# Moving the last routing chunk's steps among the first expert list's work, and a table load written ahead of them

## The chip, the cores and the metric

The kernel runs on one core of a Trainium2 chip. The core has five engines that each take their instructions in order: TensorE (PE, with its weight loads as PEld), VectorE (DVE), ScalarE (ACT), GpSimd (POOL) and SyncE (SP, which only issues DMA transfers here). They wait for one another through semaphores. The metric is the device time of one execution in microseconds, lower is better; the median of three runs of the kernel before is 774.65 us (772.66 to 775.27).

## The reference

Three layers run one after the other on 1536 tokens of width 512:

```
scores = q @ k.T / sqrt(64), kept for 4 sink columns and a window of 128
x = softmax(scores) @ v                          # 2 batches, 8 heads, 768 positions
h = x @ w_in;  x = (h - tanh(h)) @ w_out         # 512 -> 2048 -> 512
logits = x @ w_gate + log1p(exp(x @ w_noise)) * noise      # 8 experts
top2 and their softmax weights
for e in experts, k in (0, 1):                   # 512 -> 1024 -> 512 per expert
    out[mask] += weight * (relu(x[mask] @ w1[e]) @ w2[e])
```

## The kernel before, in words

**Attention** goes block by block (12 blocks of 128 tokens, 4 pairs of heads each): scores on PE (L371), masked maxima on DVE (L382), exponentials on ACT (L395), normalising on POOL (L406), transposes (L453) and the product with v (L486) on PE. ACT and DVE split the dense layer's first weights beside it: `split_d` reads the loaded tile `rawi0` on ACT (L215, into `cai0`) and on DVE (L216, L220, L223, L228).

**The dense layer** walks the list `seq` of (group, chunk, unit): `a_l1` (L606) makes a tile `h`, `a_chain` applies Tanh on ACT (L614), subtracts on DVE (L616) and splits in two parts (L619, L621), `a_l2` (L638) adds into the chunk's output. Six chunks of 256 tokens; the first four end early, chunk 4 next, chunk 5 last.

**Routing** is the generator `route(c0, c1)`. Each `next` issues one step: transposes of the chunk's rows (L695), their evacuation (L707), the logits (L720), then on DVE and ACT the noise scale (Exp at L751, Ln at L755), the two largest (L766, L768), the running counts on PE (`pp`, L782 and L785), the softmax weights (Exp at L787), positions and row data, and at the end the scatters of the rows into DRAM `xs` by POOL (L808). The last chunk's generator is `r5`; its steps are pulled by `r(k)` between the units of expert list 0.

**The experts** are lists of tokens gathered from `xs`. List 0 holds tokens of the first four chunks alone, so that its work can start while chunk 5 is still routed; lists 1 to 7 need all chunks. Unit n of a list is `b_l1(n)` (L978, tile `h`), `b_chain(n)` (Relu on ACT at L988, the low part on DVE at L989, tile `hh`) and `b_l2(n)` (L1002). There are two banks for `h`: `b_l1(n + 2)` can start when `b_chain(n)` has read its bank. Units 96 to 103 are list 0 (N1 is 96), 104 on is list 1. Its rows come by SP transfers (L903, `xr<-xs`) that wait for every scatter; DVE transposes them (L943), ACT and DVE split them (L961, L963), and then PE can start `h104`. Expert weights are loaded (`rawi<-wm`) and split on ACT and DVE (L231, L232) beside this.

**What sets the order.** Instructions are written in program order and then placed by a scheduler with priorities, engine by engine. From the last dense unit to unit N1 + 10 the order is pinned as written (`in_order`); before it, the scheduler may move an instruction forward to any place that its dependences allow. The loads of ACT's function tables are not written in this kernel: a pass behind the scheduler puts one ahead of an ACT function that the set then loaded lacks.

Of the kernel before, what the change touches and what calls it, by code (L numbers as in the profile page):

```python
# [71 lines left out]
def kernel(ctx: ExitStack, tc: tile.TileContext, qkv, vsink, w64, wm, wgn, noise, out,  # L72
# [609 lines left out]
    def route(c0, c1):  # L682
# [114 lines left out]
        V.tensor_scalar(rs, dd, 1.0, 1e-9, op0=ALU.add, op1=ALU.add)
        V.reciprocal(rs, rs)
        for c in range(c0, c1):
            x, ms = x2s[c], slice((c - c0) * CB, (c - c0 + 1) * CB)  # L800
            xi = x.bitcast(I32)
            V.tensor_copy(x[:, :, 516], ev[:, 0, ms])
            V.tensor_copy(xi[:, :, 517], sl[:, 0, ms])
            V.tensor_copy(x[:, :, 514], rs[:, ms])
            V.tensor_mul(x[:, :, 515], dd[:, ms], rs[:, ms])

# [161 lines left out]

    def b_l1(n, mid=None):
        e, u, d = b_at(n)  # L970
# [5 lines left out]
        for wa, xa in ((0, 0), (1, 0), (0, 1)):  # L976
            for k in range(4):
                nc.tensor.matmul(h[:, :width(e)], w[:, wa, k * 256 + s * P:k * 256 + (s + 1) * P],  # L978
                                 xg[e][:, k, xa, :width(e)], start=t == 0, stop=t == 11)
                t += 1  # L980
                if mid and t == 8:
                    mid()
# [447 lines left out]
```

## Time and profile before

| | |
|---|---|
| Median of 3 runs | 774.65 us (772.66 to 775.27) |
| The profiled execution's own time | 772.26 us |
| Its span, first to last instruction | 770.0 us |
| Mean granted TensorE clock | 0.979 of full speed |
| PE busy | 723.9 us (94%) |
| DVE / ACT / POOL busy | 475.9 (62%) / 356.3 (46%) / 186.4 us (24%) |
| Attention and first dense units | about 0 to 82 us |
| Dense layer (with the rest of attention) | to 425.6 us |
| List 0 | 425.6 to 456.3 us |
| Lists 1 to 7 and the last small list | 460.2 us to the end |

The profile names each instruction by line, engine, operation and tile; times count from the span's start. A line of the timeline gives start, length, the instruction, how many were merged, and in brackets the engine's idle time just before it with what ended it.

### The profile page before, as it was taken

To read this page: it belongs to the slowest core of one execution; us is meant where nothing else is said; L and a number is where in the kernel's file an instruction comes from. 1 tells how busy PE (TensorE), PEld (TensorE's weight loads), DVE (VectorE), ACT (ScalarE), POOL (GpSimd) and SP (SyncE) were. 2 spreads that over 40 slices of the span, in tenths; PEclk is the share of its full clock that TensorE was granted. 3 is DMA by queue.
4 is the path that set the end of the run, shared out by engine and by line. 5 is a ranking of instruction groups with operands and counts; after the bars stand their busy time and mean duration, and the time that the engine had idled before them with its cause. 6 is when DMAs were issued, how large, how long until landed. Compare 5 with 4: busy or idle time off the path is not lost.

```text
span 770.0 us, 12093 instructions
## 1 busy us (share of the span) xinstructions
PE 723.9 (94%) x4346; PEld 653.0 (85%) x4346; DVE 475.9 (62%) x1203; ACT 356.3 (46%) x785; POOL 186.4 (24%) x219
## 2 busy tenths in 40 slices
PE   6878999999699999999999979999999999999991
PEld 3565788888699999988888979999999999899991
DVE  5998678877587587446467766776646474544221
ACT  4977688776353344234346534444343434332110
POOL 4444355531000000000351231313131313132321
PEclk9999899999899999999999999999999999999996
DMA  7453111006998133000225388756757444444421
GB/s 263 138 178 109 56 51 61 2 1 206 297 287 233 56 110 110 1 1 1 84 112 167 125 237 237 213 164 194 193 186 192 164 155 160 143 139 165 143 84 35
DMA packets 62117, 104.96 MB, mean 136 GB/s; under 512 B 19629, under 2 KB 45869, under 8 KB 55392
## 3 DMA queue, kind: packets, MB, share of 16 engines
q1 hardware_dynamic: 54528, 80.20, 34.9%
q0 software_dynamic: 7376, 22.85, 8.7%
q10 hardware_dynamic: 144, 1.05, 0.3%
q8 instruction: 36, 0.59, 0.3%
q14 instruction: 33, 0.27, 0.1%
HBM read 79.12 MB, written 25.68 MB: 136 GB/s over the span
## 4 chain that ended last, share of the span: by engine, by line
PE 44%; issue 24%; DMA 15%; POOL 6%; DVE 6%; ACT 3%; POOLq 0%; SPq 0%; ACTq 0%; DVEq 0%
PE h L606 16%; PE acc L638 15%; DMA prev<-out,tab 6%; DMA out<-y,tab 5%; PE xb L486 4%; POOL out L1030 4%; PE s L371 3%; DMA rawo<-w 2%; POOL prev L883 2%; PE pt L453 2%; DVE e L382 1%; DMA rawi<-wm 1%; ACT e L395 1%; PE x2p L695 1%; PE y L1002 1%
## 5 line engine op out<-in xcount | busy, mean ns | idle before, releaser
L606 PE MATMUL h<-xT,wi 128*128 128x256 f32 x1152 | 160.9, 287 | 7.9 <-DVE th L616 5.9
L606 PEld LDWEIGHTS h<-xT,wi 128*128 128x128 f32 x1152 | 153.1, 192 | 14.9 <-DVE th L616 6.4
L978 PE MATMUL h<-xg,wi 128*128 128x424 f32 (+1 forms) x768 | 157.6, 354 | 4.0 <-ACT xg L961 3.9
L1002 PE MATMUL y<-hh,wo 128*128 128x424 f32 (+1 forms) x768 | 152.0, 347 | 0.7 <-DVE yt L1016 0.5
L638 PE MATMUL acc<-wo,g 128*128 128x512 f32 x576 | 151.1, 396 | 0.0
L978 PEld LDWEIGHTS h<-xg,wi 128*128 128x128 f32 x768 | 138.6, 190 | 8.7 <-ACT xg L961 5.0
L1002 PEld LDWEIGHTS y<-hh,wo 128*128 128x128 f32 x768 | 139.4, 188 | 4.1 <-DVE yt L1016 0.9
L638 PEld LDWEIGHTS acc<-wo,g 128*128 128x128 f32 x576 | 101.9, 189 | 16.5
L988 ACT ACTIVATE hh<-h 128x424 fp32r<-128x424 f32 (+1 forms) x64 | 32.6, 511 | 149.9 <-PE h L978 147.6
L1030 POOL DMA_INDIRECT out<-y,tab x33 | 41.4, 1255 | 189.7 <-DVE y L1029 189.4
L808 POOL DMA_INDIRECT xs<-x,sl x24 | 26.0, 1085 | 235.7 <-DVE th L616 183.7
L989 DVE SCALAR_TENSOR_TENSOR hh<-h,hh 128x424 fp32r<-128x424 f32 (+1 forms) x64 | 37.0, 578 | 73.9 <-ACT hh L988 69.8
L406 POOL TENSOR_TENSOR e<-e,nm 128x528 f32<-128x528 f32 (+1 forms) x48 | 50.1, 1044 | 81.3 <-DVE nm L404 45.5
L616 DVE TENSOR_TENSOR th<-h,th 128x256 f32<-128x256 f32 x96 | 40.4, 420 | 39.6 <-ACT th L614 37.1
L614 ACT ACTIVATE th<-h 128x256 f32<-128x256 f32 x96 | 36.6, 382 | 59.5 <-PE h L606 56.0
L619 ACT CAST g<-th 128x256 fp32r<-128x256 f32 x96 | 38.7, 404 | 55.0 <-PE acc L638 37.7
L395 ACT ACTIVATE e<-e,nm 128x264 f32<-128x264 f32 (+1 forms) x96 | 47.2, 492 | 22.5 <-DVE nm L382 20.3
L621 DVE TENSOR_TENSOR g<-th,g 128x256 fp32r<-128x256 f32 x96 | 43.2, 450 | 22.3 <-ACT g L619 21.4
L486 PE MATMUL xb<-pT,v 128*128 128x256 f32 x220 | 49.1, 352 | 3.6 <-DVE xT L501 2.2
L232 DVE TENSOR_TENSOR wi<-rawi,wi 128x1024 fp32r<-128x1024 f32 x32 | 39.1, 1223 | 21.6 <-ACT wi L231 21.5
L883 POOL DMA_INDIRECT prev<-out,tab x33 | 35.6, 1080 | 44.0 <-DMA out<-y,tab 34.6
L486 PEld LDWEIGHTS xb<-pT,v 128*128 128x128 f32 x220 | 33.7, 197 | 13.5 <-issue 5.3
(172 smaller groups left out, 888.8 us busy)
## 6 DMA issues: line engine op xcount, KB each, us to landing
rawi<-wm SPq DMA_DIRECT2D x31, 1024.0 KB
rawi<-w SPq DMA_DIRECT2D x8, 1024.0 KB
rawo<-w SPq DMA_DIRECT2D x8, 1024.0 KB
xs<-zrow SPq DMA_DIRECT2D x7, 1040.0 KB
xr<-xs SPq DMA_DIRECT2D x28, 224.0 KB
qr<-qkv SPq DMA_DIRECT2D x23, 256.0 KB
rawc<-wm SPq DMA_DIRECT2D x4, 1024.0 KB
out<-zero POOLq DMA_DIRECT2D x1, 3072.0 KB
```

The lines of the kernel that those rows point to most:

```text
L232: nc.vector.tensor_sub(t[:, 1], r, t[:, 0].bitcast(F32))
L395: nc.scalar.activation(e[:, h], e[:, h], AF.Exp, bias=nm[:, h, 0:1], scale=-1.0, accum_out=nm[:, h, 2:3])
L406: nc.gpsimd.tensor_mul(e, e, nm[:, :, 3:4].to_broadcast([P, 2, C]))
L486: nc.tensor.matmul(o, l, r_, start=t == 0, stop=t == len(todo) - 1)
L606: nc.tensor.matmul(h[:, :CT], w[:, wa, k * 256 + s * P:k * 256 + (s + 1) * P], x[:, k, xa, ts], start=t == 0, stop=t == 11)
L616: nc.vector.tensor_sub(th, h[:, :CT], th)
L621: nc.vector.tensor_sub(g[:, 1], th, g[:, 0].bitcast(F32))
L638: i = nc.tensor.matmul(acc[c][m], g[:, ga, m * P:(m + 1) * P], w[:, wa, s:s + 512], start=first and t == 0, stop=done and t == 2)
L883: nc.gpsimd.indirect_dma_start(out=dst, out_offset=None, in_=src[:rows], in_offset=bass.IndirectOffsetOnAxis(ap=t[:n, m, c:c + 1], axis=0) ...
L978: nc.tensor.matmul(h[:, :width(e)], w[:, wa, k * 256 + s * P:k * 256 + (s + 1) * P], xg[e][:, k, xa, :width(e)], start=t == 0, stop=t == 11)
L1002: nc.tensor.matmul(yacc[e][m][:, :width(e)], w[:, wa, s + m * P:s + (m + 1) * P], g[:, ga], start=u == 0 and t == 0, stop=u == NU2 - 1 and ...
L1030: i = nc.gpsimd.indirect_dma_start(out=out[:, :], out_offset=bass.IndirectOffsetOnAxis(ap=t[:n, m, 1:2], axis=0), in_=y, in_offset=None, b ...
```

## The change

In `route`, the softmax weights and the expert numbers are written before the positions are computed, for every chunk (they came behind). In the stretch of chunk 5, the transposes now stand behind all 12 matmuls of the first `b_l1` (behind 8 before); logits stand after 4 matmuls of the second (8 before); the first `b_chain` comes behind both; the steps of the noise scale, the largest two, the counts and the rest each come one unit earlier; and `b_chain(N1 + 1)` comes behind the step with the weights' Exp. A load of the table set that holds Exp and Ln is written at the start of the last dense unit.

```
@@ -787,22 +787,22 @@
         nc.scalar.activation(dd, dd, AF.Exp)
         yield
 
+        info = [(x2s[c], slice((c - c0) * CB, (c - c0 + 1) * CB)) for c in range(c0, c1)]
         if end:
             V.tensor_scalar(zz, ev, 0.0, float(E), op0=ALU.is_equal, op1=ALU.mult)
             V.tensor_add(ev, ev, zz)
+        V.tensor_scalar(rs, dd, 1.0, 1e-9, op0=ALU.add, op1=ALU.add)
+        V.reciprocal(rs, rs)
+        for x, ms in info:
+            V.tensor_copy(x[:, :, 516], ev[:, 0, ms])
+            V.tensor_copy(x[:, :, 514], rs[:, ms])
+            V.tensor_mul(x[:, :, 515], dd[:, ms], rs[:, ms])
         V.tensor_tensor(o12, o12, ppv[:, None].to_broadcast([P, 2, nb, E]), ALU.mult)
         V.tensor_reduce(pos, o12, axis=AX.X, op=ALU.add)
         sl = gp2.tile([P, 2, nb], I32, tag="sl", name=f"sl{c0}", bufs=2)
         V.scalar_tensor_tensor(sl, ev, float(SEC), pos, op0=ALU.mult, op1=ALU.add)
-        V.tensor_scalar(rs, dd, 1.0, 1e-9, op0=ALU.add, op1=ALU.add)
-        V.reciprocal(rs, rs)
-        for c in range(c0, c1):
-            x, ms = x2s[c], slice((c - c0) * CB, (c - c0 + 1) * CB)
-            xi = x.bitcast(I32)
-            V.tensor_copy(x[:, :, 516], ev[:, 0, ms])
-            V.tensor_copy(xi[:, :, 517], sl[:, 0, ms])
-            V.tensor_copy(x[:, :, 514], rs[:, ms])
-            V.tensor_mul(x[:, :, 515], dd[:, ms], rs[:, ms])
+        for x, ms in info:
+            V.tensor_copy(x.bitcast(I32)[:, :, 517], sl[:, 0, ms])
 
         def scatter(m, k, behind=None):
             i = nc.gpsimd.indirect_dma_start(
@@ -966,7 +966,7 @@
         e, u = divmod(n - N1, NU2)
         return e, u, 8 + e * 4 + u // 2
 
-    def b_l1(n, mid=None):
+    def b_l1(n, mid=None, at=12):
         e, u, d = b_at(n)
         w = wsp["i", d]
         s = u % 2
@@ -978,7 +978,7 @@
                 nc.tensor.matmul(h[:, :width(e)], w[:, wa, k * 256 + s * P:k * 256 + (s + 1) * P],
                                  xg[e][:, k, xa, :width(e)], start=t == 0, stop=t == 11)
                 t += 1
-                if mid and t == 8:
+                if mid and t == at:
                     mid()
 
     def b_chain(n):
@@ -1235,6 +1235,8 @@
     PAIR = N1 - 12
     for n in range(-3, N1):
         marks["a", n] = mark()
+        if n == N1 - 1:
+            nc.scalar.preload_act_table_set("natural_log_exp_and_others")
         g, c, u, d = a_at(max(n, 0))
         ch = a_chain(n + 2) if 0 <= n + 2 < N1 else iter(())
         if n + 3 < N1:
@@ -1301,29 +1303,32 @@
         for _ in range(k):
             next(r5, None)
 
...
     b_l1(N1, lambda: r(2))
+    b_l1(N1 + 1, lambda: r(2), 4)
     b_chain(N1)
-    b_l1(N1 + 1, lambda: r(2))
+    r(1)
     for n in range(N1, N):
         marks["a", n] = mark()
         e, u, d = b_at(n)
         if n == N1:
-            r(2)
-        if n == N1 + 1:
             r(1)
         edge = e == 0 and u >= NU2 - 2
-        if n + 1 < N and not (edge and u == NU2 - 1):
+        if n + 1 < N and n != N1 and not (edge and u == NU2 - 1):
             b_chain(n + 1)
         if n + 2 < N and not edge:
             need("i", b_at(n + 2)[2])
             b_l1(n + 2)
-        if n == N1 + 1:
+        if n == N1:
             r(1)
         if n >= N1 + 3 and n != N1 + 7:
             emit(1, min(d + 3, ND - 1))
         need("o", d)
         b_l2(n)
-        if n == N1 + 1:
+        if n == N1:
+            r(1)
+            b_chain(n + 1)
             r(2)
         if n == N1 + 2:
             emit(2, 11)
```

What the engines get is shown at three places, in rows of the built programs.

**Start of the program, ACT.** `e0` are scores of block 0, `nm0_p` the maxima and sums of its head pair p, `pT` the evacuated transposes, `cai0` the first step of the weight split. Before:

```order
L395 ACT_TABLE_LOAD
L395 ACTIVATE e0_0_119,nm0_0_120<-e0_0_119,nm0_0_120 128x132 x2
L395 ACTIVATE e0_0_119,nm0_1_179<-e0_0_119,nm0_1_179 128x132 x2
L395 ACTIVATE e0_2_197,nm0_2_198<-e0_2_197,nm0_2_198 128x132 x2
L395 ACTIVATE e0_2_197,nm0_3_216<-e0_2_197,nm0_3_216 128x132 x2
L458 COPY pT0_0_207<-pt0_0_0_208 128x256
L458 COPY pT0_1_225<-pt0_1_0_226 128x256
L215 ACTIVATE cai0_246<-rawi0_184 128x512
```
Now:

```order
L1239 ACT_TABLE_LOAD
L395 ACTIVATE e0_0_119,nm0_0_120<-e0_0_119,nm0_0_120 128x132 x2
L215 ACTIVATE cai0_246<-rawi0_184 128x512
L395 ACTIVATE e0_0_119,nm0_1_179<-e0_0_119,nm0_1_179 128x132 x2
L395 ACTIVATE e0_2_197,nm0_2_198<-e0_2_197,nm0_2_198 128x132 x2
L458 COPY pT0_0_207<-pt0_0_0_208 128x256
L395 ACTIVATE e0_2_197,nm0_3_216<-e0_2_197,nm0_3_216 128x132
L458 COPY pT0_1_225<-pt0_1_0_226 128x256
L215 ACTIVATE cai0_246<-rawi0_184 128x512
```
The written table load (L1239) has gone from the last dense unit to the head of the program. The first half of `cai0`, which reads the load `rawi0`, has moved from behind the transposes to behind the first pair's two exponentials, and its second half has come forward.

**First Tanh of the dense layer, ACT and PE.** `th0`, `h0` to `h3` belong to the first dense units, `wi1` is the second weight tile, `pt3_2` and `xb3_0` are transposes and value products of attention block 3. ACT before:

```order
L435 CAST st3_0_590<-s4_0_0_1_586 128x128
L226 ACTIVATE wi1_629<-czi1_631 128x512
L614 ACTIVATE th0_607<-h0_592 128x256
L226 ACTIVATE wi1_629<-czi1_631 128x512
L215 ACTIVATE cao1_665<-rawo1_627 128x512
L619 CAST g0_623<-th0_607 128x256
L614 ACTIVATE th1_644<-h1_610 128x256
```
ACT now:

```order
L435 CAST st3_0_590<-s4_0_0_1_586 128x128
L226 ACTIVATE wi1_629<-czi1_631 128x512
L614 ACT_TABLE_LOAD
L614 ACTIVATE th0_607<-h0_592 128x256
L226 ACTIVATE wi1_629<-czi1_631 128x512
L614 ACTIVATE th1_644<-h1_610 128x256
L619 CAST g0_623<-th0_607 128x256
```
PE before, from `h1`:

```order
L606 MATMUL h1_610<-xT0_72,wi0_245 128x256 x12
L606 MATMUL h2_647<-xT0_72,wi1_629 128x256 x12
L453 MATMUL pt3_2_0_697<-ident_64,e3_2_522 128x128
L606 MATMUL h3_683<-xT0_72,wi1_629 128x256 x6
L486 MATMUL xb3_0_674<-pT3_0_544,v3_393 128x256
L486 MATMUL xb3_0_674<-pT3_0_544,v2_285 128x256
L486 MATMUL xb3_0_674<-st3_0_590,vs0_232 128x256
```
PE now:

```order
L606 MATMUL h1_610<-xT0_72,wi0_245 128x256 x12
L453 MATMUL pt3_2_0_697<-ident_64,e3_2_522 128x128 x2
L486 MATMUL xb3_0_674<-pT3_0_544,v3_393 128x256
L486 MATMUL xb3_0_674<-pT3_0_544,v2_285 128x256
L606 MATMUL h2_647<-xT0_72,wi1_629 128x256 x12
L486 MATMUL xb3_0_674<-st3_0_590,vs0_232 128x256
L453 MATMUL pt3_2_0_697<-ident_64,e3_2_522 128x128
```
The first Tanh now has a table load ahead of it. On PE, two of the four transposes and two value products have moved from behind `h2` to ahead of it.

**The last chunk, ACT, DVE and PE.** `rt5`, `sm5` are the routing's tables, `hh97` and `hh98` the Relu of list 0's units. ACT before:

```order
L751 ACTIVATE rt5_4962<-rt5_4962 128x16
L755 ACT_TABLE_LOAD
L755 ACTIVATE rt5_4962<-rt5_4962 128x16
L988 ACTIVATE hh97_4973<-h97_4939 128x296
L988 ACTIVATE hh98_5009<-h98_4976 128x296
L787 ACT_TABLE_LOAD
L787 ACTIVATE sm5_4964<-sm5_4964 128x2
L988 ACTIVATE hh99_5075<-h99_5012 128x296
```
ACT now:

```order
L751 ACTIVATE rt5_4963<-rt5_4963 128x16
L755 ACT_TABLE_LOAD
L755 ACTIVATE rt5_4963<-rt5_4963 128x16
L787 ACT_TABLE_LOAD
L787 ACTIVATE sm5_4965<-sm5_4965 128x2
L988 ACTIVATE hh97_5021<-h97_4937 128x296
L988 ACTIVATE hh98_5048<-h98_4974 128x296
L988 ACTIVATE hh99_5076<-h99_5051 128x296
```
DVE before, from the difference of the two largest (L786):

```order
L786 TENSOR_TENSOR sm5_4964<-rt5_4962 128x2
L791 TENSOR_SCALAR sm5_4964<-sm5_4964 128x2x2
L792 TENSOR_TENSOR sm5_4964<-sm5_4964 128x2x2
L793 TENSOR_TENSOR rt5_4962<-rt5_4962,pp5_5034 128x2x16
L794 TENSOR_REDUCE sm5_4964<-rt5_4962 128x2x2
L796 SCALAR_TENSOR_TENSOR sl5_5055<-sm5_4964 128x4
L797 TENSOR_SCALAR sm5_4964<-sm5_4964 128x2
L798 RECIPROCAL sm5_4964<-sm5_4964 128x2
L802 COPY x2_5_2569<-sm5_4964 128x2
L803 COPY x2_5_2569<-sl5_5055 128x2
L804 COPY x2_5_2569<-sm5_4964 128x2
L805 TENSOR_TENSOR x2_5_2569<-sm5_4964 128x2
```
DVE now, from the instruction just behind that difference (L786):

```order
L989 SCALAR_TENSOR_TENSOR hh97_5021<-h97_4937,hh97_5021 128x296
L792 TENSOR_SCALAR sm5_4965<-sm5_4965 128x2x2
L793 TENSOR_TENSOR sm5_4965<-sm5_4965 128x2x2
L794 TENSOR_SCALAR sm5_4965<-sm5_4965 128x2
L795 RECIPROCAL sm5_4965<-sm5_4965 128x2
L797 COPY x2_5_2569<-sm5_4965 128x2
L798 COPY x2_5_2569<-sm5_4965 128x2
L799 TENSOR_TENSOR x2_5_2569<-sm5_4965 128x2
L800 TENSOR_TENSOR rt5_4963<-rt5_4963,pp5_5016 128x2x16
L801 TENSOR_REDUCE sm5_4965<-rt5_4963 128x2x2
L803 SCALAR_TENSOR_TENSOR sl5_5033<-sm5_4965 128x4
L805 COPY x2_5_2569<-sl5_5033 128x2
```
PE before, from `h98`:

```order
L978 MATMUL h98_4976<-xg0_4863,wi9_4737 128x296 x12
L1002 MATMUL y0_0_4989<-hh96_4936,wo8_4785 128x296 x3
L1002 MATMUL y0_1_4990<-hh96_4936,wo8_4785 128x296 x3
L1002 MATMUL y0_2_4991<-hh96_4936,wo8_4785 128x296 x3
L1002 MATMUL y0_3_4992<-hh96_4936,wo8_4785 128x296 x3
L978 MATMUL h99_5012<-xg0_4863,wi9_4737 128x296 x12
L782 MATMUL pp5_5034<-rt5_4962,tri_92 128x16
L785 MATMUL pp5_5034<-macc_95,ones_93 128x16
L1002 MATMUL y0_0_4989<-hh97_4973,wo8_4785 128x296 x3
```
PE now:

```order
L978 MATMUL h98_4974<-xg0_4863,wi9_4737 128x296 x12
L1002 MATMUL y0_0_4991<-hh96_4960,wo8_4785 128x296 x3
L1002 MATMUL y0_1_4992<-hh96_4960,wo8_4785 128x296 x3
L1002 MATMUL y0_2_4993<-hh96_4960,wo8_4785 128x296 x3
L1002 MATMUL y0_3_4994<-hh96_4960,wo8_4785 128x296 x3
L782 MATMUL pp5_5016<-rt5_4963,tri_92 128x16
L785 MATMUL pp5_5016<-macc_95,ones_93 128x16
L978 MATMUL h99_5051<-xg0_4863,wi9_4737 128x296 x12
L1002 MATMUL y0_0_4991<-hh97_5021,wo8_4785 128x296 x3
```
Both table loads of the last chunk are still there. `hh97` and `hh98` have moved on ACT from ahead of the Exp at L787 to behind it; on DVE the low part of `hh97` (L989) stands between the difference and the weights. The counts `pp5` come ahead of `h99` on PE.

## Rows read from the trace of the kernel before

**Rows 1.** The page: busy time, its share of the span and instructions by engine

```profile
PE 723.9 (94%) x4346; PEld 653.0 (85%) x4346; DVE 475.9 (62%) x1203; ACT 356.3 (46%) x785; POOL 186.4 (24%) x219
```

**Rows 2.** By stretch: length, PE, PEld, DVE, ACT, POOL busy, clock, DMA share, GB/s

```profile
20.00:42.00 22.00, 18.73 (x98) 11.56 (x96) 19.44 (x76) 20.20 (x58) 11.12 (x10) 1.00 0.37 121
42.00:82.00 40.00, 33.00 (x164) 25.07 (x165) 34.58 (x106) 27.02 (x73) 14.15 (x12) 0.87 0.44 145
82.00:182.00 100.00, 99.04 (x711) 83.87 (x711) 76.33 (x274) 75.93 (x223) 46.16 (x54) 1.00 0.12 36
54.00:58.00 4.00, 4.00 (x21) 3.91 (x21) 3.91 (x10) 2.55 (x7) 1.28 (x1) 0.57 0.42 170
64.00:74.00 10.00, 6.53 (x34) 4.33 (x31) 9.23 (x33) 7.14 (x22) 4.11 (x4) 1.00 0.42 142
460.20:469.30 9.10, 9.03 (x37) 7.97 (x38) 5.46 (x17) 4.16 (x7) 0.00 (x0) 0.81 0.88 223
```

**Rows 3.** Timeline of PE, list 0 and the start of list 1

```profile
434.91 1.90 PE L978 MATMUL h<-xg,wi 128*128 128x296 f32 x12
437.34 0.37 PE L782 MATMUL pp<-rt,tri 128*128 128x16 f32 x2 [0.53 <-DVE rt L772]
...
451.15 5.11 PE L1002 MATMUL y<-hh,wo 128*128 128x296 f32 x36
460.16 9.29 PE L978 MATMUL h<-xg,wi 128*128 128x424 f32 x36 [3.90 <-ACT xg L961]
```

**Rows 4.** Timeline of DVE just before list 1

```profile
458.88 2.23 DVE L943 STREAM_TRANSPOSE xf<-xr 128x448 f32<-128x448 f32 x4 [2.11 <-DMA xr<-xs]
```

**Rows 5.** Timeline of POOL: first and last scatter of the last chunk (four in all)

```profile
439.89 1.58 POOL L808 DMA_INDIRECT xs<-x,sl  x1 [14.25 <-issue]
...
445.07 0.97 POOL L808 DMA_INDIRECT xs<-x,sl  x1 [0.30 <-issue]
```

**Rows 6.** Timeline of DVE, last chunk's routing

```profile
431.82 0.18 DVE L749 COPY rt<-lp 128x32 f32<-128x32 f32 x1
...
435.60 0.47 DVE L989 SCALAR_TENSOR_TENSOR hh<-h,hh 128x296 fp32r<-128x296 f32 x1
...
437.51 0.15 DVE L786 TENSOR_TENSOR sm<-rt 128x2 f32<-128x2 f32 x1
...
438.96 0.15 DVE L805 TENSOR_TENSOR x<-sm 128x2 f32<-128x2 f32 x1
```

**Rows 7.** Timeline of ACT, last chunk's routing

```profile
432.24 0.21 ACT L751 ACTIVATE rt<-rt 128x16 f32<-128x16 f32 x1 [1.60 <-DVE rt L750]
432.47 1.28 ACT L755 ACT_TABLE_LOAD   x1
433.77 0.21 ACT L755 ACTIVATE rt<-rt 128x16 f32<-128x16 f32 x1
433.89 0.70 ACT L988 ACTIVATE hh<-h 128x296 fp32r<-128x296 f32 x2
```

**Rows 8.** Timeline of ACT, start of the program

```profile
8.72 0.40 ACT L395 ACTIVATE e<-e,nm 128x132 f32<-128x132 f32 x1 [0.32 <-DVE nm L382]
...
13.78 0.67 ACT L215 ACTIVATE cai<-rawi 128x512 f32<-128x512 f32 x1
...
21.35 0.52 ACT L395 ACTIVATE e<-e,nm 128x264 f32<-128x264 f32 x1
```

**Rows 9.** Timeline of DVE: its first reading of the load rawi

```profile
11.72 0.43 DVE L216 TENSOR_SCALAR czi<-rawi 128x512 int32<-128x512 int32 x1
```

**Rows 10.** DMA view from 0 to 16 us: rate in 40 equal slices

```profile
GB/s 0 0 0 0 76 108 96 67 334 346 310 160 138 225 202 273 300 321 440 370 330 470 351 430 389 451 410 410 451 430 358 369 389 389 394 403 364 366 350 352
```

**Rows 11.** Timeline of PE, first dense units and attention between them

```profile
53.74 2.33 PE L606 MATMUL h<-xT,wi 128*128 128x256 f32 x12 [1.99 <-ACT wi L226]
...
57.36 1.28 PE L486 MATMUL xb<-pT,v 128*128 128x256 f32 x4
...
66.44 1.10 PE L486 MATMUL xb<-pT,v 128*128 128x256 f32 x4 [1.85 <-DVE xT L501]
```

More of the change, by code (lines that the diff above doesn't have):

```diff
@@ L788, in route @@
         yield
+        info = [(x2s[c], slice((c - c0) * CB, (c - c0 + 1) * CB)) for c in range(c0, c1)]
         if end:
@@ L792, in route @@
             V.tensor_add(ev, ev, zz)
+        V.tensor_scalar(rs, dd, 1.0, 1e-9, op0=ALU.add, op1=ALU.add)
+        V.reciprocal(rs, rs)
+        for x, ms in info:
+            V.tensor_copy(x[:, :, 516], ev[:, 0, ms])
+            V.tensor_copy(x[:, :, 514], rs[:, ms])
+            V.tensor_mul(x[:, :, 515], dd[:, ms], rs[:, ms])
         V.tensor_tensor(o12, o12, ppv[:, None].to_broadcast([P, 2, nb, E]), ALU.mult)
@@ L796, in route @@
         V.scalar_tensor_tensor(sl, ev, float(SEC), pos, op0=ALU.mult, op1=ALU.add)
[L797 to L805, printed above, removed]
+        for x, ms in info:
+            V.tensor_copy(x.bitcast(I32)[:, :, 517], sl[:, 0, ms])
         def scatter(m, k, behind=None):
@@ L967, in b_at, with b_l1 @@
         return e, u, 8 + e * 4 + u // 2
-    def b_l1(n, mid=None):
+    def b_l1(n, mid=None, at=12):
         e, u, d = b_at(n)
@@ L980, in b_l1 @@
                 t += 1
-                if mid and t == 8:
+                if mid and t == at:
                     mid()
@@ L1237 @@
         marks["a", n] = mark()
+        if n == N1 - 1:
+            nc.scalar.preload_act_table_set("natural_log_exp_and_others")
         g, c, u, d = a_at(max(n, 0))
@@ L1304 @@
     b_l1(N1, lambda: r(2))
+    b_l1(N1 + 1, lambda: r(2), 4)
     b_chain(N1)
-    b_l1(N1 + 1, lambda: r(2))
+    r(1)
     for n in range(N1, N):
@@ L1310 @@
         if n == N1:
-            r(2)
-        if n == N1 + 1:
             r(1)
         edge = e == 0 and u >= NU2 - 2
-        if n + 1 < N and not (edge and u == NU2 - 1):
+        if n + 1 < N and n != N1 and not (edge and u == NU2 - 1):
             b_chain(n + 1)
@@ L1319 @@
             b_l1(n + 2)
-        if n == N1 + 1:
+        if n == N1:
             r(1)
@@ L1325 @@
         b_l2(n)
-        if n == N1 + 1:
+        if n == N1:
+            r(1)
+            b_chain(n + 1)
             r(2)
```

## Prediction

> **What bounds the kernel now.** I read the page's busy line first: PE is at work for 723.9 us, 94% of the span [rows 1], so some 46 us of idle PE and some slow clock are all that an edit of the order can win. The windows by stretch say where the edited places lie. From 82 to 182 us PE works 99.04 of 100 us at clock 1.00; from 42 to 82 us it works 33.00 of 40, and from 20 to 42 us ACT (20.20 of 22) and DVE (19.44) are the fuller engines [rows 2]. So the start, to 82 us, is set by attention and the weight split on ACT and DVE, and a delay there passes on to the dense part, which has no slack to take it back.
>
> The last chunk's place is read from PE's timeline backwards: list 0 ends at 451.15 + 5.11 = 456.26, then PE is idle for 3.90 us until ACT has split list 1's rows, and `h104` starts at 460.16 [rows 3]. What ends last before it: DVE, which waited for the gathered rows (`xr`) until 458.88 [rows 4]; those wait for the last chunk's four scatters, 439.89 to 445.07 + 0.97 = 446.04 [rows 5]; the first scatter starts 0.78 us behind the last write of its rows, 438.96 + 0.15 = 439.11 [rows 5, 6]. So list 1 starts when the routing's chain lets it, not when PE comes free. The last scatter's end to `h104` is 460.16 − 446.04 = 14.1 us, which the edit doesn't touch. The wait costs a second thing: from 460.20 to 469.30 us the granted clock is 0.81 [rows 2], so 9.1 × 0.19 = 1.7 us go by at the lower level.
>
> **The change part by part.** The sum is made against the profiled execution's own 772.26 us (span 770.0, and 2.26 around it); the median shown is 774.65, or 2.39 above, and I add that at the end.
>
> *The noise scale.* The chunk's Exp (L751) starts at 432.24 behind an ACT that had been idle for 1.60 us [rows 7]; it can come at most that much earlier. Its input is made by DVE from 431.82 on [rows 6]. In the new order the logits stand 4 matmuls behind `h96`'s twelve, and DVE's L749 no longer stands behind a weight cast: following the new order by the old durations, L749 comes at 430.5, 1.3 us earlier. Ln follows with its table load (1.28 us, 432.47 to 433.77) still ahead of it [rows 7], so it too gains 1.3.
>
> *Up to the difference of the two largest (L786).* Two low parts of list 0's units, 0.47 us each with about 0.38 of it not overlapped, leave the way to L786: another 0.6 (a little is lost to waits). L786 comes at 437.51 − 1.3 − 0.6 = 435.6 [rows 6].
>
> *The weights and positions.* Here the order gives back. `hh97` stands on ACT behind the Exp at L787, and its low part on DVE stands ahead of the weights. The Exp's table load follows Ln at once and is over before L786; the Exp ends at about 435.95, the first Relu (half of the 0.70 of [rows 7]) at 436.3, the low part at 436.85. Behind it come the eleven small steps that before took from 437.51 to 439.11, 1.60 us [rows 6]; that the weights come ahead of the positions adds none and takes none. Their last write is at 436.85 + 1.55 = 438.4, a gain of 0.7 and not of 1.9. Bounds: −1.9, if DVE isn't held by `hh97`, and +0.3, if a further wait of 1 us comes in front of that Relu. I take −0.7, as the steps between are all rows of before. The same 0.7 goes to the scatters and, over an unchanged 14.1 us, to `h104`: 459.45.
>
> *List 0 itself.* It has no bearing on that as long as it ends before 459.45. `pp` stands ahead of `h99` now and `h99` needs the bank of `hh97`, which is read until 436.85: PE waits there for 1 to 1.5 us where it waited 0.53 before [rows 3], and list 0 ends at 457.0 to 457.4. PE's wait before list 1 shrinks from 3.90 to about 2.3 us, but 0.9 of that is only moved ahead.
>
> *The clock behind the wait.* A wait of 1.99 us at 53.74 [rows 11] is followed by clock 0.57 from 54 to 58 us; one of 1.85 us at 66.44 [rows 11] by clock 1.00 throughout 64 to 74 us [rows 2]. The new wait of 2.3 is longer than both; the clock may fall or not, 0 or −1.7. I take that it still falls, a gain of 0: the nearest row by length, 1.99, was followed by the lower clock.
>
> *The table load written ahead.* The order of ACT shows it at the head of the program, where a load of the other set stood (nothing is won or lost there), and so it is not there for the last chunk: both loads stay, and the first Tanh gets a load of its own. By the row of Ln's load that is 1.28 us [rows 7], for ACT at 52.8 us, just where PE waits 1.99 us for ACT's weight split (`wi`) [rows 11]. The load delays `wi` and so `h2` by 0 to 1.28 us. Against it, PE has two transposes and two value products moved ahead of `h2`, into that wait; four products take 1.28 [rows 11], so some 1 us of work fills it: −1.6 (all of it and the lower clock behind it) to 0. I take 0 for the two together, with −1.6 and +1.28 as ends. The Trainium skill ("ScalarE: Activation LUTs", What ACT_TABLE_LOAD costs) gives a switch of sets 1283 ns and about 1380 ns of drain. The trace agrees on the first and shows none of the second: the Ln starts 0.02 us behind its load's end [rows 7]. By that page this term would be 1.4 us dearer, and the sum 1.4 higher.
>
> *The start of the program.* What the edit didn't name is the dearest: the scheduler has put half of `cai0` ahead of the exponentials of head pair 1 on ACT. These exponentials run at 8.72 and `cai0` at 13.78 [rows 8]. `cai0` reads the load `rawi0`. DVE reads it first at 11.72 [rows 9]; before that five tiles of attention's inputs (1.31 MB) and its own 1.05 MB must come, 2.36 MB, and the DMA view's slices add up to 2.29 MB at 10.0 us and 2.47 at 10.4 [rows 10]. So it lands between 10.0 and 11.72, and ACT, which takes its instructions in order, stands until then. Pair 1 runs at 10.6 to 12.3 in place of 8.72: +1.9 to +3.6, less the 0.67 of `cai0` that is no longer due at 13.78 [rows 8]: +1.2 to +3.0 at that place. From there to the exponential of 21.35 [rows 8] ACT has gaps, and behind it 22 − 20.20 = 1.8 us of idle time to 42 us [rows 2]; these can take back from nothing to all. I take +1.2, the lower end of the place itself, with 0 and +3.0 as bounds.
>
> *Sum:* +1.2 (start) + 0 (Tanh's load against the filled wait) − 0.7 (chain) + 0 (clock) = +0.5: 772.8 for such an execution, 774.65 + 0.5 = 775.2 as a median.
>
> **The rivals.** *A, the forecast:* 775.2.
> *B, faster: the start is absorbed and the clock stays up.* ACT's gaps take the whole delay of `cai0`, the filled wait at `h2` gives 0.6, the chain 0.7, and the wait before list 1 is short enough for the full clock, 1.7: −3.0, 771.65. For it: ACT's 1.8 us idle behind the delay, and the 1.85-us wait without a fall. Against it: DVE takes its instructions in order behind the sums of pair 1, and the 1.99-us wait with a fall.
> *C, slower: the wait for `rawi0` isn't taken back.* It lands at 11.7, DVE, 19.44 of 22 us busy, has no room, and the dense part starts 3.0 later; Tanh's load costs 0.6 net; less 0.7: +2.9, 777.55. It decides from the point where the exponential of 21.35 comes 2.5 us or more late. For it: DVE's first reading is at 11.72 [rows 9]. Against it: that instruction stood behind others on DVE, so its start is no proof of a late landing.
> *D, the load ahead does what it says:* Ln's load off the chain, −1.28: 773.9. Against it stands the order, in which both loads are left.
>
> **How the numbers follow.** A 0.46, B 0.28, C 0.24, D 0.02. About 0.3%, 2.3 us, is what a measurement of this kernel can tell from no change. A and D are within it, B and C outside, on either side: faster 0.28, same 0.48, slower 0.24. The range reaches past B and C by the little that the median may be off, 771.2 to 778.2; A's own is 774.0 to 777.0 (its start at 0 and at +3.0).
>
> **What would show it.** Right: ACT's `cai0` stands at 10 to 11.7 us with pair 1's exponentials behind it; a table load at the first Tanh and two in the last chunk; L786 some 1.9 us earlier but the last write of the rows only 0.7, with `hh97`'s low part between; PE waiting for `pp` or for `h99`; a wait of about 2.3 us before list 1. All of the last chunk is to be read against the end of the dense layer, which itself shifts by the start's term. Wrong: pair 1's exponentials where they were (then the start's term is nothing), a list 0 that ends behind the splitting of list 1's rows (then PE is the bound there and the chain's gain is lost), or a first scatter that doesn't move with the last write. Whether the clock of the 9 us behind list 1's start is near 0.81 or 1.00 decides between A and B.

## The result, and the profile after

The changed kernel takes 782.42 us (median of 17 runs, 776.66 to 789.08), the kernel before 773.25 us (17 runs, 766.57 to 777.30): a ratio of 1.0111, 95% interval 1.0081 to 1.0141. Runs more than 1.5% above the fastest of their kernel count as slow and stay out of the ratio: here one, of 789.08 us. By the ratio the kernel is slower by some 8.6 us; 775.2 us was forecast, with a range up to 778.2. The profiled execution of the changed kernel took 777.30 us, near the lower end of its runs; a second profile of it (e11 below, 784.46 us) shows the same places with larger numbers.

First the page's busy line after, in answer to [rows 1]:

```profile
PE 726.5 (94%) x4346; PEld 653.3 (84%) x4346; DVE 475.1 (61%) x1203; ACT 357.4 (46%) x786; POOL 185.7 (24%) x219
```

ACT has one instruction more (the load at the first Tanh), and the engines' work is nearly unchanged. So the loss is waiting, and a slower PE for a while. The windows by stretch, columns as in [rows 2] (the last two stretches are those behind PE's waits before list 1 and within list 0):

```profile
20.00:42.00 22.00, 20.11 (x81) 11.40 (x80) 17.84 (x69) 16.66 (x50) 8.90 (x8) 1.00 0.30 104
42.00:82.00 40.00, 33.09 (x176) 24.50 (x176) 35.42 (x113) 30.98 (x83) 16.21 (x14) 0.96 0.43 147
82.00:182.00 100.00, 98.18 (x704) 82.88 (x703) 77.20 (x281) 76.42 (x226) 47.22 (x54) 1.00 0.11 33
466.00:474.20 8.20, 7.97 (x37) 6.99 (x38) 4.86 (x16) 3.08 (x6) 0.00 (x0) 1.00 0.88 254
442.90:446.00 3.10, 3.10 (x13) 3.10 (x14) 1.65 (x11) 0.00 (x0) 0.69 (x1) 0.53 0.02 5
```

From 20 to 42 us ACT did 16.66 us of work where it did 20.20 before, PE 81 matmuls where it did 98, though PE was busy for longer: each matmul took longer. The timeline of ACT says why the start is behind:

```profile
7.40 0.39 ACT L395 ACTIVATE e<-e,nm 128x132 f32<-128x132 f32 x1
...
11.38 0.66 ACT L215 ACTIVATE cai<-rawi 128x512 f32<-128x512 f32 x1 [3.49 <-DMA rawi<-w]
11.94 0.39 ACT L395 ACTIVATE e<-e,nm 128x132 f32<-128x132 f32 x1
...
25.85 0.51 ACT L395 ACTIVATE e<-e,nm 128x264 f32<-128x264 f32 x1 [1.04 <-DVE nm L382]
```

`cai0` waits 3.49 us for its load, and head pair 1's exponentials come at 11.94 in place of 8.72 [rows 8], 3.2 us late. But the thirteenth exponential, at 21.35 before, is 4.5 us late, and the first dense matmul (L606) starts at 48.84 in place of 42.94: 5.9. Where it grows is seen on PE's timeline, the changed kernel first and then the kernel before:

```profile
10.05 0.81 PE L371 MATMUL s<-kF,qr 64*128 64x132 f32 x4
14.96 0.69 PE L453 MATMUL pt<-ident,e 128*128 128x128 f32 x2 [4.10 <-POOL e L406]
...
27.46 1.25 PE L371 MATMUL s<-kF,qr 64*128 64x264 f32 x4
...
30.06 0.72 PE L371 MATMUL s<-kF,qr 64*128 64x264 f32 x4
...
48.84 0.72 PE L606 MATMUL h<-xT,wi 128*128 128x256 f32 x4
```

```profile
18.92 1.25 PE L371 MATMUL s<-kF,qr 64*128 64x264 f32 x4
...
21.75 0.71 PE L371 MATMUL s<-kF,qr 64*128 64x264 f32 x4
...
42.94 0.72 PE L606 MATMUL h<-xT,wi 128*128 128x256 f32 x4
```

The same four score matmuls take 1.25 us up to a point and 0.71 from there on. Before, the point lies between 19 and 22 us; in the changed kernel, where PE stood still for 4.10 us, it lies between 27 and 30. So PE works some 9 us longer at the slower rate. The column of the granted clock reads 1.00 in both stretches, but the trace has no record of the clock that early: the first one, at 1.00, begins at 20.31 us before and at 29.39 in the changed kernel, just where the lengths change. Ahead of it the lengths are those of the lower level, 1.2 GHz: a 128x128 transpose (L453) of the kernel before takes 0.42 us there, 0.42 too in the low stretch of 54 to 58 us [rows 2], and 0.27 where the clock is recorded at 1.00.

Of the 5.9 us at the first dense matmul 3.7 are left at 160 us and 4.1 at the end of the dense layer, where `h96` starts. Part of what came back goes with the clock of this one execution: from 42 to 82 us it was 0.96 here and 0.87 before [rows 2]. In e4 below, with 0.87 in the same stretch, 7.1 us at the first dense matmul are still 7.2 at `h96`. The start of `h96`, the changed kernel and then the kernel before:

```profile
429.71 0.58 PE L978 MATMUL h<-xg,wi 128*128 128x296 f32 x3
```

```profile
425.63 1.25 PE L978 MATMUL h<-xg,wi 128*128 128x296 f32 x8
```

The rest of the loss is in the last chunk, where PE's timeline answers to [rows 3]:

```profile
441.38 0.37 PE L782 MATMUL pp<-rt,tri 128*128 128x16 f32 x2 [1.62 <-DVE rt L772]
...
442.88 3.21 PE L978 MATMUL h<-xg,wi 128*128 128x296 f32 x12 [0.91 <-DVE hh L989]
...
459.19 5.14 PE L1002 MATMUL y<-hh,wo 128*128 128x296 f32 x36
466.02 8.21 PE L978 MATMUL h<-xg,wi 128*128 128x424 f32 x36 [1.69 <-ACT xg L961]
```

PE waits 1.62 + 0.91 = 2.53 us for `pp` and for `h99`'s bank (0.53 before). Behind these two waits the clock is 0.53 (about the lower level, 1.2 GHz) from 442.90 to 446.00 us, and `h99` takes 3.21 us where it took 1.90 [rows 3]. List 0 so ends 34.62 us behind `h96`'s start (30.63 before) and list 1 starts 36.31 behind it (34.53 before), 1.8 later and not 0.7 earlier.

Two things are late there. One is list 0 itself. Before, DVE had waited 2.11 us for the gathered rows when it began to transpose them [rows 4]; now it comes to them straight from copying out list 0's last outputs (L1016). These are the last of the four scatters on POOL, and then DVE:

```profile
449.89 0.97 POOL L808 DMA_INDIRECT xs<-x,sl  x1 [0.30 <-issue]
```

```profile
464.37 0.47 DVE L1016 COPY yt<-y 128x296 f32<-128x296 f32 x1 [0.37 <-PE y L1002]
464.75 2.21 DVE L943 STREAM_TRANSPOSE xf<-xr 128x448 f32<-128x448 f32 x4
```

From the last scatter's end to list 1 it is 15.2 us in place of 14.1 [rows 3, 5], and no longer the rows but list 0's end sets list 1's start. The other is the routing's chain, whose last write comes 1.3 us later against `h96`. ACT and then DVE show why, in answer to [rows 6, 7]:

```profile
435.64 1.05 ACT L231 CAST wi<-rawi 128x1024 fp32r<-128x1024 f32 x1 [2.06 <-DMA rawi<-wm]
436.59 0.21 ACT L751 ACTIVATE rt<-rt 128x16 f32<-128x16 f32 x1
436.82 1.28 ACT L755 ACT_TABLE_LOAD   x1
438.11 0.22 ACT L755 ACTIVATE rt<-rt 128x16 f32<-128x16 f32 x1
```

```profile
435.34 0.19 DVE L749 COPY rt<-lp 128x32 f32<-128x32 f32 x1 [1.17 <-PE lp L720]
...
436.72 1.22 DVE L232 TENSOR_TENSOR wi<-rawi,wi 128x1024 fp32r<-128x1024 f32 x1 [0.97 <-ACT wi L231]
437.86 0.17 DVE L754 TENSOR_SCALAR rt<-rt 128x16 f32<-128x16 f32 x1
...
441.56 0.15 DVE L786 TENSOR_TENSOR sm<-rt 128x2 f32<-128x2 f32 x1
442.36 0.47 DVE L989 SCALAR_TENSOR_TENSOR hh<-h,hh 128x296 fp32r<-128x296 f32 x1 [0.65 <-ACT hh L988]
...
444.37 0.17 DVE L805 COPY x<-sl 128x2 int32<-128x2 int32 x1
```

The Exp stands on ACT behind the cast of the weight tile `wi11` (L231), which waits 2.06 us for its load; on DVE the other half of that split (L232) stands ahead of L754. Neither has to do with the routing. L786, the difference of the two largest, comes 11.85 us behind `h96`'s start, as before (11.88), and from L786 to the last write of the rows it is 2.98 us (444.54 − 441.56), before 1.60 [rows 6], of which 0.65 is the wait for `hh97`.

In the table all times are starts (the last write and list 0: ends) less the start of that kernel's `h96`, from the profiled execution of each:

| | L749 | Exp L751 | Ln L755 | L786 | last write | list 0 ends | list 1 starts |
|---|---|---|---|---|---|---|---|
| before | 6.19 | 6.62 | 8.14 | 11.88 | 13.49 | 30.63 | 34.53 |
| changed | 5.63 | 6.88 | 8.40 | 11.85 | 14.83 | 34.62 | 36.31 |
| e11, changed again | 6.25 | 7.72 | 9.24 | 12.70 | 15.69 | 36.80 | 38.49 |
| e2 no load | 5.92 | 7.17 | 8.69 | 11.81 | 14.80 | 33.33 | 36.31 |
| e3 load pinned | 4.95 | 6.55 | 8.02 | 11.17 | 14.16 | 34.20 | 35.89 |
| e6 before, load pinned | 8.18 | 8.60 | 9.06 | 12.84 | 14.45 | 31.60 | 34.95 |
| e7 = e6, late cast | 5.48 | 5.92 | 6.38 | 10.15 | 12.54 | 29.69 | 32.80 |
| e8 = e3, late cast | 4.95 | 5.39 | 5.85 | 9.00 | 11.99 | 30.51 | 33.38 |
| e9 = e8, chain back | 4.93 | 5.37 | 5.83 | 9.32 | 11.27 | 29.74 | 32.31 |
| e10 before, late cast | 5.48 | 5.92 | 7.44 | 11.18 | 12.79 | 29.94 | 33.82 |

One profile is a thin basis for this. Five have the last chunk in the order of before (before, e1, e4, e5, e6): list 1 starts at 33.84 to 35.83 us in them, and the cast of `wi11` on ACT at 3.8 to 6.0. Four have the changed order with that cast in it (changed, e11, e2, e3): 35.89 to 38.49. The two groups part, but only just. Behind list 1's start, which the edit leaves alone, the profiles last 296.5 to 304.5 us, with the order of before or without it; so the time of a profiled execution says little of an edit, and the medians decide.

### The profile page after: what moved, and what is told of

The parts are those of the page before. It is cut to its first block, busy times and chain, and to the rows that moved or that the text cites. A ratio compares the mean times of both kernels' runs of the same rounds, so it can differ in the third digit from the quotient of the medians.

```text
span 775.3 us, 12089 instructions
## 1 busy us (share of the span) xinstructions
PE 726.5 (94%) x4346; PEld 653.3 (84%) x4346; DVE 475.1 (61%) x1203; ACT 357.4 (46%) x786; POOL 185.7 (24%) x219
## 5 line engine op out<-in xcount | busy, mean ns | idle before, releaser
L606 PE MATMUL h<-xT,wi 128*128 128x256 f32 x1152 | 160.7, 286 | 6.0 <-DVE th L616 6.0
L606 PEld LDWEIGHTS h<-xT,wi 128*128 128x128 f32 x1152 | 153.0, 192 | 13.0 <-DVE th L616 6.4
L989 DVE SCALAR_TENSOR_TENSOR hh<-h,hh 128x424 fp32r<-128x424 f32 (+1 forms) x64 | 37.0, 578 | 72.0 <-ACT hh L988 71.8
L621 DVE TENSOR_TENSOR g<-th,g 128x256 fp32r<-128x256 f32 x96 | 41.5, 432 | 22.4 <-ACT g L619 21.7
L232 DVE TENSOR_TENSOR wi<-rawi,wi 128x1024 fp32r<-128x1024 f32 x32 | 39.0, 1222 | 26.2 <-ACT wi L231 26.1
```

What stands on the lines that cost most here:

```text
L232: nc.vector.tensor_sub(t[:, 1], r, t[:, 0].bitcast(F32))
L606: nc.tensor.matmul(h[:, :CT], w[:, wa, k * 256 + s * P:k * 256 + (s + 1) * P], x[:, k, xa, ts], start=t == 0, stop=t == 11)
L621: nc.vector.tensor_sub(g[:, 1], th, g[:, 0].bitcast(F32))
```

## The experiments

The theory (T): the written load, alone, reorders the start; ACT then waits for `rawi0`, and most of the loss is there. The rival (U): the loss is in the last chunk. The first four kernels part the two. Without the written load every row up to the last chunks' routing is again that of before; with it alone, the start is the changed kernel's.

**e1, the written load alone**, in the kernel before:

```
     for n in range(-3, N1):
         marks["a", n] = mark()
+        if n == N1 - 1:
+            nc.scalar.preload_act_table_set("natural_log_exp_and_others")
```

> The kernel before with the written table load alone. The load floats to the head of the program and the order of attention's start is the changed kernel's (half of cai0 ahead of head pair 1 on ACT, a load at the first Tanh); the last chunk is as before. Theory T (the loss sits at the start): pair 1's exponentials come about 3 us late as in the changed kernel, the delay reaches 5 to 6 us at 40 us, and this kernel alone carries the whole loss, 779 to 785 us, ratio 1.008 to 1.014. Rival U (the profiled pair shows +4.1 at the end of the dense layer and the rest in the last chunk): at most half, ratio 1.003 to 1.006.

Ratio 1.0076 (1.0040 to 1.0112), 780.64 us. Its ACT timeline:

```profile
12.14 0.66 ACT L215 ACTIVATE cai<-rawi 128x512 f32<-128x512 f32 x1 [4.26 <-DMA rawi<-w]
12.71 0.39 ACT L395 ACTIVATE e<-e,nm 128x132 f32<-128x132 f32 x1
```

`cai0` starts 0.8 us later here than in the changed kernel, and the first dense matmul is 7.8 us late, `h96` 5.6. (The profiled execution, 786.35 us, is among the slowest of its runs; 7.5 us of its loss lie behind list 1's start.) Of the change's 1.11%, 0.76 sits in this one line, and at the start: T, by size and place. The kernels with this order of the start (changed, e1, e4, e11) have `h96` at 429.71 to 432.81 us; those that have the start of before, and their first exponential at 7.5 us as it had (before, e3, e7, e8, e9), at 423.87 to 425.76.

**e2, the changed kernel without the written load:**

```
-        if n == N1 - 1:
-            nc.scalar.preload_act_table_set("natural_log_exp_and_others")
```

> The changed kernel without the written load: the start is exactly the order of before, the last chunk's reordering is there, its two loads are on ACT as before. T: about the time of before, ratio 0.998 to 1.002 (my blind -0.7 us for the chain, ratio 0.999). U: slower by 2 to 4 us, ratio 1.003 to 1.006, with the last write of the rows later against the end of the dense layer (+1.3 us in the changed kernel's trace) and list 0 ending later.

Ratio 1.0028 (0.9992 to 1.0063), 776.24 us: between the two, and the interval holds no change. The trace is plainer than the time: the last write comes at 14.80 us in place of 13.49 and list 1 1.8 us later (table). My −0.7 us for the chain isn't there. PE's two waits are 1.31 and 0.91 us, but the clock doesn't fall behind them (`h99` takes 1.90), list 0 ends at 33.33, and DVE waits 1.20 us for the rows: here the rows, and with them the routing's chain, set list 1's start. e1 and e2 add up to 0.76% + 0.28% = 1.04%, of the change's 1.11.

**e3, the load pinned**, in the changed kernel:

```
-            nc.scalar.preload_act_table_set("natural_log_exp_and_others")
+            after(nc.scalar.preload_act_table_set("natural_log_exp_and_others"), 1)
```

> The changed kernel with the written load held behind the ACT instruction written before it: it now stands behind the last Tanh's work, ahead of the last chunk's evacuation L707, both loads of the last chunk are gone, the start is that of before. T: the start's loss is gone and Ln follows the Exp without 1.28 us of load, so the last write comes about 1.3 earlier than in e2: ratio 0.996 to 1.000. U: the load only moves ahead of L707 on the same chain and PE waits for pp and h99 as before, so the same as e2.

Ratio 1.0010 (0.9978 to 1.0043), 774.24 us. The start's loss is gone, but that both loads are gone from the last chunk brings Ln nothing. On ACT and on DVE:

```profile
430.52 1.05 ACT L231 CAST wi<-rawi 128x1024 fp32r<-128x1024 f32 x1 [2.42 <-DMA rawi<-wm]
431.48 0.21 ACT L751 ACTIVATE rt<-rt 128x16 f32<-128x16 f32 x1
432.95 0.22 ACT L755 ACTIVATE rt<-rt 128x16 f32<-128x16 f32 x1 [1.26 <-DVE rt L754]
```

```profile
431.60 1.23 DVE L232 TENSOR_TENSOR wi<-rawi,wi 128x1024 fp32r<-128x1024 f32 x1 [1.33 <-ACT wi L231]
432.75 0.17 DVE L754 TENSOR_SCALAR rt<-rt 128x16 f32<-128x16 f32 x1
```

Where the table load of 1.28 us stood, ACT now waits 1.26 us for L754, which stands on DVE behind the cast of `wi11`. The load had hidden that wait. As in the changed kernel, the clock falls behind PE's waits (`h99` takes 3.18 us), and list 1 starts 1.69 us behind list 0's end.

**e4, another set at the head.** As e1, with the set that holds Exp and Tanh, so that the first Tanh needs no load:

```
+            nc.scalar.preload_act_table_set("exp_and_others")
```

> The kernel before with a written load of the set that holds Exp and Tanh, so that no load comes at the first Tanh; the load also floats to the head, and half of cai0 again stands ahead of head pair 1 on ACT. It parts the order of the start from the 1.28 us load at the Tanh. If the order of cai0 makes the loss: as e1, 778 to 784 us, ratio 1.007 to 1.013. If the Tanh's load and what was moved around it make it: the ratio stays within 0.998 to 1.004.

Ratio 1.0089 (1.0053 to 1.0124), 781.66 us; `cai0` waits until 11.70 and the first dense matmul is 7.1 us late. The intervals of e1 and e4 overlap: the Tanh's load is not what costs.

**e5, the cast held.** e1 with `cai0` (by the edit each of its halves) kept behind the ACT instruction written before it:

```
+                if not wide and kind == 'i' and d == 0:
+                    after(j_, 1)                 # j_: cai0's activation (L215)
```

> e1 (the written load alone, at the head of the program, the first Tanh with a load of its own), but the first half of cai0 is held behind the ACT instruction written before it, so that ACT has all four head pairs' exponentials of block 0 ahead of it. The other rows of the start are not those of before either. If ACT's wait for the load rawi0 makes the loss: the exponentials of pair 1 are back at 8 to 9 us, the exponential that was at 21.35 comes at most 1.5 us later than there, and the ratio falls from 1.008 to 1.000 to 1.004 (the Tanh's load stays). If other moves of the start make it: the ratio stays at 1.006 to 1.011.

Ratio 0.9991 (0.9955 to 1.0027), 774.52 us: all of e1's loss is gone, with the written load at the head and the Tanh's load in place. ACT's timeline (in this kernel the lines behind L215 are numbered two higher):

```profile
8.23 0.41 ACT L397 ACTIVATE e<-e,nm 128x132 f32<-128x132 f32 x1 [0.31 <-DVE nm L384]
...
13.97 0.65 ACT L215 ACTIVATE cai<-rawi 128x512 f32<-128x512 f32 x1
```

Pair 1 is at 8.23 and `cai0` no longer waits. PE's long wait (4.87 us in e1) is gone too: from 8 to 50 us none is above 0.83. The first record of the clock begins at 19.49 us, and the first dense matmul starts at 41.06 (50.73 in e1). This shows the mechanism: one instruction that waits for a load, put ahead of work that was ready.

**The last chunk.** The next kernels ask what bounds its chain, once the start is out of the way. **e6** is the kernel before with e3's pinned load:

```
+        if n == N1 - 1:
+            after(nc.scalar.preload_act_table_set("natural_log_exp_and_others"), 1)
```

> The kernel before with the written load held behind the last Tanh's work and nothing else: both loads of the last chunk go, every other row of every engine stands as before. On DVE the cast of wi11 (L232) stands ahead of L749 here, so nothing is between the Exp and L754. Theory: Ln follows the Exp at 0.5 us in place of 1.5, the last write of the rows comes about 1 us earlier against the end of the dense layer (12.5 against 13.5), and list 1 starts 1 us earlier: ratio 0.998 to 1.000. Rival (the scatters or the clock take it back): 1.000 to 1.002.

Ratio 0.9992 (0.9965 to 1.0020). Ln follows the Exp at 0.46 us, as expected, but in this profile the whole chain is late: L749 at 8.18, behind the cast of `wi11`, whose load landed late:

```profile
429.08 1.05 ACT L231 CAST wi<-rawi 128x1024 fp32r<-128x1024 f32 x1 [2.82 <-DMA rawi<-wm]
431.74 0.22 ACT L751 ACTIVATE rt<-rt 128x16 f32<-128x16 f32 x1 [1.60 <-DVE rt L750]
432.20 0.22 ACT L755 ACTIVATE rt<-rt 128x16 f32<-128x16 f32 x1 [0.24 <-DVE rt L754]
```

The removal of the two loads alone is worth nothing that can be measured here; the interval holds a gain of 2.7 us as well as a loss of 1.6.

**e7** writes the split of `wi11` later, which unit 6 of list 0 is the first to need:

```
-            emit((1, 1, 1, 1, 1, 1, 0)[n - N1 + 7], 11)
+            emit((1, 1, 1, 1, 1, 0, 0)[n - N1 + 7], 11)
...
-            emit(2, 11)                          # behind unit N1 + 2
+            emit(3, 11)
```

> e6 with the split of wi11 (L231 on ACT, L232 on DVE) written after list 0's third unit, and no longer among the routing's Exp. Theory (in e2 and e3 the chain stood behind these casts, and these behind the load rawi11): L749 comes at 5 us behind the dense layer's end in place of 6.2, the last write at about 11.3 in place of 13.5, list 1 starts 2 us earlier: ratio 0.996 to 0.999. Rival (the chain waits for something else, or the later casts collide with those of wo10 and wo11): as e6, 0.998 to 1.001.

Ratio 0.9941 (0.9911 to 0.9971), 770.64 us. ACT's timeline again:

```profile
430.53 0.22 ACT L751 ACTIVATE rt<-rt 128x16 f32<-128x16 f32 x1 [2.79 <-DVE rt L750]
430.99 0.21 ACT L755 ACTIVATE rt<-rt 128x16 f32<-128x16 f32 x1 [0.24 <-DVE rt L754]
```

The Exp waits for the routing alone. List 1 starts 32.80 us behind `h96`, 1.7 earlier than before. The last write came 1.2 later than I had expected, since L793 waits 0.79 us for `pp`, which stands behind `h99` in this order.

**e8**, the changed kernel with pinned load and late cast, and **e9**, the same with the second unit's chain back where it was:

> e3 (the whole change with the load pinned) with the split of wi11 written after list 0's third unit. Theory: L754 no longer waits for the cast of wi11, Ln comes at about 6 us behind the dense layer's end in place of 8.0, L786 at 9.2 in place of 11.2, PE's waits for pp (1.64) and h99 (0.91) shrink to under 1 us together, last write at about 12.0: ratio 0.996 to 0.999. Rival (the order with hh97 behind the Exp is what makes PE wait): PE's two waits stay at 2 to 2.5 us, ratio 0.999 to 1.003.

```
-        if n + 1 < N and n != N1 and not (edge and u == NU2 - 1):
+        if n + 1 < N and not (edge and u == NU2 - 1):
             b_chain(n + 1)
...
-            r(1)
-            b_chain(n + 1)
-            r(2)
+            r(3)
```

> e8 with the second unit's chain (hh97) written back ahead of the third b_l1, as in the kernel before: its Relu stands ahead of L787's Exp again and its low part ahead of L760, and no longer between L786 and the weights. Theory: L786 comes 0.4 us later than in e8 (9.4 us behind the dense layer's end), but the last write follows it at 1.65 us in place of 3.0, at 11.0 us; h99 finds its bank free; list 1 starts 0.9 us earlier than in e8 (32.5 us): ratio 0.992 to 0.996. Rival (PE's wait for list 1 only grows and the lower clock takes it back): 0.995 to 0.998, as e8.

e8: 0.9953 (0.9923 to 0.9984), 771.79 us; PE waits 0.61 us for `h99`'s bank in place of 2.53 in all, so that it was the late chain, and not `hh97`'s place alone, that had made PE wait. e9: 0.9962 (0.9933 to 0.9992), 770.32 us. PE then waits nowhere in list 0:

```profile
433.06 0.33 PE L782 MATMUL pp<-rt,tri 128*128 128x16 f32 x2
...
433.46 1.87 PE L978 MATMUL h<-xg,wi 128*128 128x296 f32 x12
...
456.18 10.44 PE L978 MATMUL h<-xg,wi 128*128 128x424 f32 x36 [2.56 <-ACT xg L961]
```

So the steps that the change moved do shorten the chain, to 11.27 us (12.54 in e7, with the order of before), once the cast is out of it and `hh97` isn't between L786 and the weights. But of list 1's start 2.2 us earlier, the 36 matmuls behind the wait take 1.15 back (10.44, before 9.29 [rows 3]).

**e10, the late cast alone:** e7's edit of the two `emit` lines, in the kernel before.

> The kernel before with the late split of wi11 alone; both table loads stay on ACT as before. It parts e7 into its two edits. If the casts and the load rawi11 behind them held the chain: L749 at 5.5 us behind the dense layer's end in place of 6.2, but Ln 1.5 behind the Exp because of its table load, last write about 12.8 (before 13.5, e7 12.5): ratio 0.996 to 0.999. If e7's gain needed both edits: as before, 0.999 to 1.001.

Ratio 0.9953 (0.9920 to 0.9986), 770.35 us. The gain of e7 to e9 is there with both table loads in place: it is the cast. Its size isn't accounted for: the time falls by 3.6 us (1.1 to 6.2), while list 1 starts 0.7 us earlier than in the profile of before and at most 2.0 earlier than in the other four with that order. The intervals of e7 to e10 overlap; which of them is best isn't settled, and all four beat both kernels.

**e11, the changed kernel again**, with no edit, for a second profile:

> The changed kernel once more, with a profile, on the chip of these runs, since its profiled run (777.3) lies below its median (782.4). Theory: the exponentials of pair 1 stand behind cai0 at 11.4 to 12.2 us again, the first dense matmul comes 6 to 8 us late, and the time is 777 to 787 us.

784.46 us, within what was expected. Pair 1 stands behind `cai0` at 12.02, the first dense matmul is 7.1 us late, `h96` 5.7, and the last chunk adds 4.0 (38.49 against 34.53):

```profile
443.85 0.37 PE L782 MATMUL pp<-rt,tri 128*128 128x16 f32 x2 [1.86 <-DVE rt L772]
...
445.34 3.33 PE L978 MATMUL h<-xg,wi 128*128 128x296 f32 x12 [0.89 <-DVE hh L989]
448.47 2.99 PE L1002 MATMUL y<-hh,wo 128*128 128x296 f32 x12
```

Here `h99` and the twelve behind it both run at the lower clock (3.33 and 2.99). List 0 ends at 36.80, and list 1 again starts 1.69 us behind that.

## Why the prediction was wrong

**The start of the program, +1.2: the step that failed.** The place was right: `cai0` waits to 11.38 (10.0 to 11.7 was the estimate; 11.70 to 12.14 in e4, e11 and e1), and pair 1 comes 3.2 us late (1.9 to 3.6; up to 4.0 in e1). What failed is "ACT has gaps" that "can take back from nothing to all", and taking the lower end of the place itself with +3.0 as the bound. The delay didn't shrink on ACT; it became a wait of 4.10 us on PE, and PE ran at the lower clock for some 9 us more. In changed, e1, e4 and e11, the four profiles with this order, the first dense matmul was 5.9, 7.8, 7.1 and 7.1 us late, and `h96` 4.1, 5.6, 7.2 and 5.7. As a time the term is e1's 0.76%, some 5.9 us, and e5 shows that it goes with `cai0`'s place.

That the longer stretch at the lower clock makes the growth from 3.2 to 5.9 us is argued and not shown, as no kernel here moves that stretch alone. In e3 and e9, with the same start, its end lies 5.7 us apart (24.61 and 18.95) and the first dense matmul 0.9; in e3 and before, 4.3 and 1.4 (in e9 and before, 1.4 apart, the earlier end has the later matmul, by 0.4). By the first two pairs the 9.1 us of the changed kernel (29.39 and 20.31) would cost 1.5 to 2.9 us, an estimate, of the 2.7.

Rival C had the wait and its condition (2.5 us late at the exponential of 21.35; measured 4.5), with a price of half the size and nothing of PE's clock. Bounds that add up one engine's delay left out what PE does when it stands still.

**The Tanh's load and the filled wait, 0:** the load is there (1.28 us, the Tanh 0.02 us behind it), and e4, without it, is no faster than e1. The Trainium skill ("ScalarE: Activation LUTs", What ACT_TABLE_LOAD costs) adds about 1380 ns of drain to such a switch; the trace shows none here either:

```profile
58.78 1.28 ACT L614 ACT_TABLE_LOAD   x1
60.08 0.38 ACT L614 ACTIVATE th<-h 128x256 f32<-128x256 f32 x1
```

**The noise scale, −1.3, and L786, −1.9: wrong.** "L749 no longer stands behind a weight cast" was true, and L749 comes 0.6 us earlier (1.2 in e3, but 0.1 later in e11). But the cast had only moved ahead of the next step, on DVE of L754, and its ACT half was ahead of the Exp all along. So the Exp came 0.3 us later against `h96` and not 1.3 earlier, and L786 at 11.85 us, where it had been at 11.88, and not 1.9 earlier. I took the 1.60 us in which ACT was idle as free; it was free because that load had landed early in the one profile that I read. Behind `h96` this cast started at 4.0 us before, at 5.9 in the changed kernel, at 5.6 in e3 and at 6.0 in e6.

**The weights and positions, behind `hh97`: right in mechanism and size.** From L786 to the last write it was 2.98 us where I had 2.8 (438.4 − 435.6). With the line above it makes +1.3 and not −0.7.

**List 0, no bearing: wrong.** PE's waits were 2.53 us (1 to 1.5 forecast; with these the end of list 0 should have read 456.7 to 457.2, and not 457.0 to 457.4). The clock fell behind them in the changed kernel, e11 and e3, though not in e2; I had looked for that only behind the longer wait before list 1. `h99` lost 1.3 us by it. In those three profiles list 0's end, and not the rows, set list 1's start: the 14.1 us from the last scatter on, taken as unchanged, were 15.2, 16.4 and 15.4.

**The clock before list 1, 0:** the wait was 1.69 us (2.3 forecast); the 36 matmuls behind it took 8.21 us in one profile of the changed kernel, at clock 1.00, and 9.78 in the other behind the same 1.69. It goes either way. (The forecast's 1.7 us is what the low clock costs; the time spent at the lower level is about twice that.)

**Rival D** was rightly out: both loads stayed. In the changed order its −1.28 was not to be had either (e3); in the order of before e6's interval leaves it open.

## What to carry to other kernels

When an order changes, look first for instructions that wait for a transfer and have come ahead of ready work on their engine: the price is the wait until the transfer has landed, and it doesn't stay on that engine if the others starve. When a stretch is taken to have no bearing as long as it ends early enough, work out how much later it may end before it sets the pace. When a replay by old durations says that a step comes earlier, ask of each neighbour ahead of it when its own load lands, in more than one profile. In this kernel a written line without any dependence went where the scheduler liked; pin it, and compare the whole program's order, not the place that was edited.

## What the runs showed of the hardware that I had not expected

PE starts the program at the lower clock: the same four matmuls take 1.25 and later 0.71 us, and the trace's first record of the clock begins at that step. Between kernels with the same start the step comes at different times, at 18.95 us in e9 and at 24.61 in e3, and with it the first dense matmul at 43.37 or 44.31. In the four profiles with the early `cai0` it comes at 29.39 to 32.54 us. Short waits can be followed by the lower clock: in the changed kernel two of 1.62 and 0.91 us close to one another were; in e2 two of 1.31 and 0.91 us were not.
